# Loads tied to steps of the unit ahead, DMA transposes for units 4 to 10, and new constants in the planner of a fused attention and ReLU-squared kernel

## The chip, the cores and the metric

The kernel runs on one core of one Trainium2 chip. The metric is the device time in microseconds (us) of one execution; lower is better. The inputs and the output lie in HBM as fp32.

## The reference

Two layers follow one another. The first is a gated linear attention over 4 batches, 8 heads, 768 tokens and a head size of 48; the second is a dense block on all 3072 tokens, with 384 inputs, 2048 hidden values and 384 outputs.

```python
for t in range(S):                       # per batch b and head h
    state = alpha[:, :, t, :, None] * state + einsum('bhd,bhe->bhde', k[:, :, t], v[:, :, t])
    y[:, :, t] = einsum('bhd,bhde->bhe', q[:, :, t], state)
x = y.transpose(0, 2, 1, 3).reshape(B * S, H * D)
out = (np.maximum(x @ w_in, 0) ** 2) @ w_out
```

## The kernel before

The work is cut into 12 **units**, numbered g = 0 to 11. A unit is 256 tokens of one batch, all heads; `units = [(b, i) for i in range(NST) for b in range(B)]` takes the first 256 tokens of all four batches, then the second, then the third. For each unit the program adds the following steps, each with a name that the text uses:

- **Loads** `lda`, `ldk`, `ldq`, `ldv`: alpha, k, q and v of the unit, 384 KB each, into one of four `RAW` buffers (L509; unit 0 loads alpha in two halves at L500). Those of unit 1 in part and of unit 2 in whole are issued by POOL, together with the weights `win0`, `win1`, `wout0`, `wout1` (L479); all others are issued by SP. From unit 4 on, the loads of unit g wait until q of unit g-1 has landed (`AFTER`).
- **Front**: the decays. `pr` multiplies pairs of alpha (L618/L620), `ln` and `lm` take logarithms on ACT, `m1i` and `m1s` (L627 to L631) sum them with a triangular matrix on PE, `ei`, `ea`, `ec`, `es` are exponentials on ACT, `bk` and `lb` are small steps on DVE or POOL; `ekm` and `eqm` (DVE, L689) scale k and q; `vc` casts v to bf16.
- **Transposes of scaled k and q**, `tr0` and `tr1`: by PE for units 0 to 2 (L703), by a DMA transpose that SP issues for units 3 to 11 (L716).
- **Scores** `p` (PE, L822) into the PSUM tiles psX and psZ, and the two mask steps `mk0`, `mk1` (DVE, L835).
- **Output** `y` (PE, L759 and L766), which for units 2 to 10 also holds the state products `kv` of the next unit (L739); `sa`, `sb`, `sc`, `sd` update the state. `xe` copies the attention output out of psX (L853/L855).
- **Transpose of the attention output**, `xt`, into one of four `XT` buffers. For units 0 to 7 it is done by PE, in six 128x128 transposes into psX (L868), and `xv` copies the result (DVE, L880). For units 8 to 11 SP issues one DMA transpose (L874) and there is no `xv`.
- **Dense block**: `s1_g_u`, eight groups of six matmuls (L925), reads `XT` and `WIN` and fills one of two PSUM banks; `re` applies the ReLU (ACT L933 or DVE L935), `sq` squares (L943/L947). `s2_g_j_s`, eight groups of four matmuls (L961), multiplies with `WOUT` into the one bank psO; `oe` copies it out (ACT L968 or DVE L970) and `out` stores it (SP, L971). The last 128 rows go through `last_tile` (L895 to L903).

No loop of the kernel sets the order in which these steps stand on an engine. The class `Program` collects them with their reads, writes, estimated durations (`cost`) and priorities (`prio`, built from `FRONT`, `ATTN` and `DENSE`, or 13000 ns times g where a unit has no entry). Its `schedule` plays the steps through with its own constants (`HOP`, the delay of a semaphore; `PE_LATENCY`; `SWITCH`, 95 ns for a change of PE's mode; the DMA constants) and gives every engine a fixed list. A step that has several engines open to it (`alts`) goes to the one that the planner finds free first. `fill` then puts dummy matmuls on PE (L1005, one is 128x256 with zeros) into gaps of over 250 ns that the planner expects before the first `s2`. `place` works out which semaphores each step waits for. On the chip every engine, SP among them, runs its list in that order, and a step that waits holds up all that stands behind it on its engine.

The mode of a PE step, a pair for its beginning and its end, is known to the planner alone: F for steps on the whole array, R for `kv`, T for `p`. Where the mode changes, the planner adds `SWITCH` and may prefer another step of the present mode.

Of the kernel before, what the change touches and what calls it, by code (L numbers as in the profile page):

```python
# [33 lines left out]
class Program:  # L34

    HOP = 70
    PE_LATENCY = 165
    DMA_FIRST = {"sp": 1300, "act": 1300, "pool": 2000}  # L40
    PACKET = (("win", 172), ("wout", 490), ("ld", 22), ("tr", 18), ("xt", 18), ("out", 65))
    SBUF_ONLY = ("pr", "bk", "aq", "ekm", "eqm", "sq", "sb", "sd")
# [58 lines left out]
    def schedule(self):  # L101
# [38 lines left out]
        def land(op, t):  # L140
            op.land = t
            for u in op.users:
# [4 lines left out]
                elif u.deps[op] or e not in u.alts:  # L147
                    ready = t + self.HOP
                else:
# [63 lines left out]
    def fill(self, make, cost, until, gap, after, cold):  # L213


        new = []
        t = after.land + self.HOP
        cold += t
# [115 lines left out]
def bass_gla_recurrent__then__act_relu_squared_kernel(  # L334
# [18 lines left out]
    G = B * NST  # L353
    units = [(b, i) for i in range(NST) for b in range(B)]
    PE_TRANSPOSED = 3
    PE_X = 8
    FRONT = {0: 0, 1: 13000, 2: 26000}
    ATTN = {}
    DENSE = {}
    POOL_LOADS = {1: "v", 2: "akqv"}  # L360
    RATIO = 4
    NRAW, NQKS, NKQT, NPM, NV, NXT, NGT, NRR, NOSB = 4, 3, 3, 2, 4, 4, 2, 4, 4
# [50 lines left out]
    pr = Program(nc)  # L413
    add = pr.add
# [17 lines left out]
    for i in range(2):  # L432
        add("dve", fill(LAF[i][:, :, :, D:64].rearrange("p j h d -> p (j h) d"), 0.0), 250, -1e6 - 10,
            writes=[("laf", i)])
        add("dve", fill(LAB[i][:, :, D:64], 0.0), 150, -1e6 + 20, writes=[("lab", i)])
    for i in range(NQKS):
        add("dve", fill(QKS[i][:, :, :, :, D:64].rearrange("p a j h d -> p (a j h) d"), 0.0), 500, -1e6 + 10,
            writes=[("qks", i, 0), ("qks", i, 1)])
# [8 lines left out]
    for part, key, val in ((HSEL[0:1, 64:128], "hsel", -1000.0), (HSEL[32:33, 0:64], "hsel", -1000.0),  # L447
# [5 lines left out]
        writes=[("ident",)])  # L453

    for c, key in enumerate(("caus", "caus1")):
        add("pool", select(flat[c], ALU.is_ge, 0.0, 128 * c, [[-1, 2], [1, 2], [2, 64]], -2), 400, -1e6 + 7,
            reads=[(key,)], writes=[(key,)])
    add("act", lambda e: e.activation(flat[1][0:64], flat[0][0:64], AF.Copy), 400, -1e6 + 8,
        reads=[("caus",), ("caus1",)], writes=[("caus1",)])
# [23 lines left out]
    load_op = {}  # L483

    def hd(ap):
        return ap.rearrange("p (h d) -> p h d", h=H)

    def load(g):
        b, i = units[g]
        t0 = i * T  # L490
        p0 = g * P
        r, la, qs, kt, pm, vb, x2 = (g % n for n in (NRAW, 2, NQKS, NKQT, NPM, NV, 2))
        first, last = i == 0, i == NST - 1
        sr, sw = 2 * b + i % 2, 2 * b + (i + 1) % 2

        for x in range(2) if g in BY_HEADS else ():
            hs = slice(4 * x, 4 * x + 4)
            src = alpha[b, hs, t0:t0 + T, :].rearrange("h (p j) d -> p h (j d)", j=2)
            dst = RAW[r][:, 0, hs].rearrange("p h j d -> p h (j d)")
            add("sp", lambda e, dst=dst, src=src: e.dma_start(dst, src), 600, L_PRIO[g] + x * 0.5,  # L500
                writes=[("raw", r, 0, x)], name=f"lda{x}_{g}", dma=f"a{r}{x}", lag=615)
        for j, t, nm in ((0, alpha, "a"), (1, k, "k"), (2, q, "q"), (3, v, "v"))[g in BY_HEADS:]:
            src = t[b, :, t0:t0 + T, :].rearrange("h (p j) d -> p h (j d)", j=2)
            dst, key = RAW[r][:, j], ("raw", r, j)
            ring, cost, gate = "sp", 600, AFTER.get((g, nm), AFTER.get(g))
            if nm in POOL_LOADS.get(g, ""):
                ring, cost = "pool", 930
            dst = dst.rearrange("p h j d -> p h (j d)")
            load_op[g, nm] = add(ring, lambda e, dst=dst, src=src: e.dma_start(dst, src), cost, (L_PRIO[g] + j if ring == "sp" else W_PRIO[2] + 10 * g + j),  # L509
                writes=[key], name=f"ld{nm}{g}", dma=f"{nm}{r}{ring}", lag=1230,  # L510
                after=[load_op[gate]] if gate else [])

    def front_by_heads(g, p0):

# [290 lines left out]
    def scores(g):  # L805

        p0 = ATTN.get(g, g * P)
        kt, pm = g % NKQT, g % NPM
# [32 lines left out]
    def output(g, with_state):  # L841
        p0 = ATTN.get(g, g * P)
        x2 = g % 2
        run, cost, reads, writes = output_mm(g)
        if with_state:
            run2, cost2, reads2, writes2 = state_mm(g + 1)
            both = lambda pe, run=run: (run(pe), run2(pe))[1]
            add("pe", both, cost + cost2, p0 + 5600, reads=reads + reads2, writes=writes + writes2, name=f"y{g}",
                mode=("F", "R"))
            state(g + 1, alone=False)  # L850
        else:
            add("pe", run, cost, p0 + 5600, reads=reads, writes=writes, name=f"y{g}", mode=("F", "R"))
        add("act", lambda e: e.activation(XBF[x2][:], psX[:, :, 0:HD], AF.Copy), act_ns(2 * HD), p0 + 6100,  # L853
            reads=[("ps", "X", 0), ("ps", "X", 1)], writes=[("xbf", x2)], name=f"xe{g}",
            alts={"dve": (lambda e: e.tensor_copy(XBF[x2][:], psX[:, :, 0:HD]), dve_ns(2 * HD))})  # L855


        s = g % NXT
        src = XBF[x2][:].rearrange("p c n -> p (c n)")
        dst = XT[s][:].rearrange("p k j t -> p (k j t)")  # L860
        bank = psX[:, 0, :].bitcast(BF16)
        to = bank[:, 0:KT * T].rearrange("p (k j c t) -> p c k j t", k=KT, j=2, c=2)

        def xtr(pe):
            for c in range(2):
                for kk in range(KT):
                    o = c * KT + kk
                    ins = pe.matmul(to[:, c, kk], src[:, o * 128:(o + 1) * 128], IDENT[:], is_transpose=True)  # L868
            return ins

        if g >= PE_X:

            to = XT[s][:].rearrange("p k j t -> p (k j t)").rearrange("p (a t) -> p a t", t=128)
            add("sp", lambda e: e.dma_start_transpose(to, src), 1300, p0 + 6700, reads=[("xbf", x2)],  # L874
                writes=[("xt", s)], name=f"xt{g}", dma=f"x{s}", lag=1400)
            return

        add("pe", xtr, pe_ns(6, 128), p0 + 6700, reads=[("xbf", x2), ("ident",)], writes=[("ps", "X", 0)],
            name=f"xt{g}")
        add("dve", lambda e: e.tensor_copy(dst, bank[:, 0:KT * T]), dve_ns(KT * T, 2),  # L880
            p0 + 7200, reads=[("ps", "X", 0)], writes=[("xt", s)], name=f"xv{g}",
            alts={"act": (lambda e: e.activation(dst, bank[:, 0:KT * T], AF.Copy), act_ns(KT * T))})
# [23 lines left out]
    def moe(g):  # L906
# [3 lines left out]
        p0 = DENSE.get(g, g * P + 20500)  # L910
        nb = FT // per
        for u in range(nb):
            hb, rb, half = h_i[0] % 2, h_i[0] // 2 % NRR, h_i[0] % 2
            h_i[0] += 1
            pu = p0 + u * P * 0.5 / nb

            def s1(pe, u=u, hb=hb):
                for i in range(per):
                    fj = u * per + i
                    for kk in range(KT):  # L920
                        mov = XT[s][:, kk].rearrange("p j t -> p (j t)")
                        if g >= PE_X:
                            mov = XT[s][:].rearrange("p k j t -> p (k j t)").rearrange(
                                "p (c k j t) -> p k j c t", c=2, k=KT, j=2)[:, kk]
                        ins = pe.matmul(psH[hb][:, i * T:(i + 1) * T], WIN[:, kk, hidden(fj)], mov,  # L925
                                        start=(kk == 0), stop=(kk == KT - 1))
                return ins

            fjs = range(u * per, (u + 1) * per)
            add("pe", s1, pe_ns(KT * per, T), pu, reads=[("xt", s)] + sorted({("win", f // FS) for f in fjs}),  # L930
                writes=[("ps", "H", hb)], name=f"s1_{g}_{u}")
            rr = RR[rb][:, half]
            add("act", lambda e, hb=hb, rr=rr: e.activation(rr, psH[hb], AF.Relu), act_ns(512), pu + 600,  # L933
                reads=[("ps", "H", hb)], writes=[("rr", rb, half)], name=f"re{g}_{u}",
                alts={"dve": (lambda e, hb=hb, rr=rr: e.tensor_scalar(rr, psH[hb], 0.0, None, ALU.max),  # L935
                              dve_ns(512))})
            if half == 0 and u < nb - 2:
                continue

            k = 2 if half == 1 and u < nb - 2 else 1  # L940
            dst = GT[gt][:, (u + 1 - k) * per:(u + 1) * per].rearrange("p f j t -> p (f j t)")
            sq = RR[rb][:, half + 1 - k:half + 1].rearrange("p a t -> p (a t)")
            add("dve", lambda e, dst=dst, sq=sq: e.tensor_tensor(dst, sq, sq, ALU.mult), 148 + k * 267, pu + 1200,  # L943
                reads=[("rr", rb, h) for h in range(half + 1 - k, half + 1)],
                writes=[("gt", gt, fj) for fj in range((u + 1 - k) * per, (u + 1) * per)], name=f"sq{g}_{u}",
                alts={"pool": (lambda e, dst=dst, sq=sq: e.tensor_tensor(dst, sq, sq, ALU.mult), 200 + k * 840),
                      "act": (lambda e, dst=dst, sq=sq: e.activation(dst, sq, AF.Square), act_ns(k * 512))})  # L947
        for j in range(2):
# [7 lines left out]
            for sg in range(4):  # L956
                ps_ = p0 + P * 0.5 + 600 + (j * 4 + sg) * P * 0.5 / 8

                def s2(pe, sg=sg, j=j, psS=psS):
# [6 lines left out]
                    reads=[("gt", gt, fj) for fj in range(sg * FT // 4, (sg + 1) * FT // 4)] + [("wout", sg * WS // 4)],  # L966
                    writes=[keyS], name=f"s2_{g}_{j}_{sg}")
            add("act", lambda e, ob=ob, psS=psS: e.activation(OSB[ob][:], psS, AF.Copy), act_ns(DM), ps_ + 700,  # L968
                reads=[keyS], writes=[("osb", ob)], name=f"oe{g}_{j}",
                alts={"dve": (lambda e, ob=ob, psS=psS: e.tensor_copy(OSB[ob][:], psS), dve_ns(DM))})  # L970
            add("sp", lambda e, ob=ob, rows=rows: e.dma_start(out[rows, :], OSB[ob][:]), 600, ps_ + 1300,  # L971
                reads=[("osb", ob)], name=f"out{g}_{j}", dma=f"o{ob}", lag=600)
# [18 lines left out]
    for st in ORDER:  # L991
        kind, g = st[0], int(st[1:])
# [44 lines left out]
```

## Time and profile before

| | before |
|---|---|
| median of 7 runs | 180.3 us (179.91 to 181.14) |
| profiled execution, its own time | 180.38 us |
| its span, first to last instruction | 178.6 us |
| granted TensorE clock | 1.00 |
| busy: PE, PE weight loads, DVE, ACT, POOL | 173.5, 138.3, 121.4, 119.4, 27.9 us |
| SP's DMA queue (q1), share of 16 engines | 63.9% |
| POOL's DMA queue (q0), share of 16 engines | 12.8% |

Busy time is the sum of an engine's instructions in the profile. Matmuls overlap in the record (the next starts before the one ahead has ended), so the work of a PE step is read from the distance between its first start and that of the next step, not from its duration. 1.78 us of the profiled execution lie outside its span.

### The profile page before, as it was taken

The page shows a single profiled execution, that of the slowest core. Times are in us where ns is not written, and L with a number is a line of the kernel's source. Part 1 is how long each engine was busy: PE and PEld are TensorE (multiplying, and loading weights), DVE is VectorE, ACT ScalarE, POOL GpSimd, SP SyncE. Part 2 cuts the span into 40 slices and gives each one's busy share as a digit, 9 for nine tenths or more (in the row PEclk, how much of TensorE's full clock was granted, in tenths as well). Part 3 has the DMA queues.
Part 4 walks back from the last instruction along what each step waited for, and adds up shares of the span by engine and source line. Part 5 has one row for each costly group of instructions (what it writes and reads, how often), then busy time and mean ns, then how long its engine had stood idle before and what let it go on. Part 6 is the DMA issues. An engine that isn't in the chain of part 4 may idle for free.

```text
span 178.6 us, 5262 instructions
## 1 busy us (share of the span) xinstructions
PE 173.5 (97%) x2309; PEld 138.3 (77%) x2309; DVE 121.4 (68%) x197; ACT 119.4 (67%) x214; POOL 27.9 (16%) x35
## 2 busy tenths in 40 slices
PE   7999799999999999999999999999999999999994
PEld 5877698876788788878778878688878787788773
DVE  6579488589867997987889796974738645424130
ACT  5584399598777868949657869566559454656441
POOL 3250751020020301503304331000000000000000
DMA  5999999999999998799999999236132541130112
GB/s 131 305 298 191 215 308 211 238 257 269 248 282 229 299 308 237 180 263 286 258 189 323 223 265 287 74 66 145 48 77 48 132 48 44 48 88 0 46 45 88
DMA packets 72215, 32.59 MB, mean 182 GB/s; under 512 B 67488, under 2 KB 70688, under 8 KB 72192
## 3 DMA queue, kind: packets, MB, share of 16 engines
q1 hardware_dynamic: 70544, 27.14, 63.9%
q0 software_dynamic: 1648, 5.11, 12.8%
q8 instruction: 18, 0.29, 0.7%
q14 instruction: 5, 0.04, 0.1%
HBM read 25.17 MB, written 4.72 MB: 167 GB/s over the span
## 4 chain that ended last, share of the span: by engine, by line
PE 88%; DMA 8%; SPq 2%; issue 0%; ACT 0%
PE psWH L925 37%; PE psO L961 34%; DMA win<-in_moe_w_in_dram 5%; PE psX L766 3%; DMA raw<-in_alpha_dram 3%; PE psX L759 3%; PE psZ L739 2%; PE psX L822 2%; SPq L509 2%; PE psX L895 1%; PE psZ L822 1%; PE psX L868 1%; PE psWH L627 1%; PE psO L1005 1%; SPq L500 1%; PE psZ L703 0%
## 5 line engine op out<-in xcount | busy, mean ns | idle before, releaser
L925 PE MATMUL psWH<-xt,win 128*128 128x256 bf16 x576 | 74.0, 275 | 1.2 <-DMA win<-in_moe_w_in_dram 1.2
L925 PEld LDWEIGHTS psWH<-xt,win 128*128 128x128 bf16 x576 | 65.1, 145 | 6.2 <-issue 1.4
L961 PE MATMUL psO<-wout,gt 128*128 128x384 bf16 x368 | 69.1, 326 | 0.0
L933 ACT ACTIVATE rr<-psWH 128x512 bf16<-128x512 f32 x84 | 49.9, 596 | 25.0 <-PE psWH L925 23.2
L961 PEld LDWEIGHTS psO<-wout,gt 128*128 128x128 bf16 x368 | 34.7, 98 | 18.1 <-DVE gt L943 0.2
L943 DVE TENSOR_TENSOR gt<-rr 128x1024 bf16<-128x1024 bf16 (+1 forms) x42 | 24.6, 589 | 27.1 <-ACT rr L933 26.7
L968 ACT ACTIVATE osb<-psO 128x384 f32<-128x384 f32 x21 | 10.3, 492 | 13.8 <-PE psO L961 13.5
L835 DVE TENSOR_TENSOR pm<-psZ,caus 128x1024 bf16<-128x1024 f32 x12 | 14.6, 1216 | 4.0 <-PE psZ L822 4.0
L835 DVE TENSOR_TENSOR pm<-psX,caus 128x1024 bf16<-128x1024 f32 x12 | 14.6, 1219 | 2.8 <-PE psZ L822 2.8
L947 ACT ACTIVATE gt<-rr 128x1024 bf16<-128x1024 bf16 (+1 forms) x18 | 15.5, 864 | 0.7 <-DVE rr L935 0.4
L1005 PE MATMUL psO<-zero 128*128 128x256 bf16 x76 | 12.3, 310 | 1.2 <-DVE zero L426 1.2
L620 POOL TENSOR_TENSOR prd<-raw 128x384 f32<-128x384 f32 x7 | 7.6, 1088 | 35.2 <-DMA raw<-in_alpha_dram 35.2
L853 ACT ACTIVATE xbf<-psX 128x768 bf16<-128x768 f32 x10 | 8.1, 809 | 6.8 <-PE psZ L739 5.4
L689 DVE TENSOR_TENSOR qks<-raw,ek 128x768 bf16<-128x768 f32 x11 | 10.5, 951 | 0.1
L689 DVE TENSOR_TENSOR qks<-raw,eq 128x768 bf16<-128x768 f32 x11 | 10.5, 950 | 0.0
L935 DVE TENSOR_SCALAR rr<-psWH 128x512 bf16<-128x512 f32 x12 | 8.3, 688 | 2.8 <-PE psWH L925 2.5
L1005 PEld LDWEIGHTS psO<-zero 128*128 128x128 bf16 x76 | 7.9, 110 | 2.9 <-DVE zero L426 1.2
L766 PE MATMUL psX<-vbf,pm 64*128 64x48 bf16 x384 | 6.9, 180 | 0.0
L792 DVE TENSOR_TENSOR tmp<-psZ,sbd 128x384 f32<-128x384 f32 x8 | 4.4, 552 | 3.4 <-PE psZ L739 3.4
L685 POOL CAST vbf<-raw 128x768 bf16<-128x768 f32 x4 | 4.6, 1153 | 13.3 <-DMA raw<-in_v_dram 10.3
L639 ACT ACTIVATE ek<-psWH 128x384 f32<-128x384 f32 x10 | 4.9, 489 | 2.1 <-PE psWH L627 1.1
L766 PEld LDWEIGHTS psX<-vbf,pm 64*128 64x128 bf16 x384 | 5.6, 93 | 0.8
(119 smaller groups left out, 170.7 us busy)
## 6 DMA issues: line engine op xcount, KB each, us to landing
out_dram<-osb SPq DMA_DIRECT2D x23, 192.0 KB, 3.4
raw<-in_k_dram SPq DMA_DIRECT2D x11, 384.0 KB, 4.5
raw<-in_q_dram SPq DMA_DIRECT2D x11, 384.0 KB, 5.0
raw<-in_v_dram SPq DMA_DIRECT2D x10, 384.0 KB, 5.1
raw<-in_alpha_dram SPq DMA_DIRECT2D x10, 384.0 KB, 4.4
win<-in_moe_w_in_dram POOLq DMA_DIRECT2D x2, 768.0 KB, 10.1
wout<-in_moe_w_out_dram POOLq DMA_DIRECT2D x2, 768.0 KB, 9.1
raw<-in_v_dram POOLq DMA_DIRECT2D x2, 384.0 KB, 5.7
```

Of the source, the lines that this page charges most:

```text
L689: add("dve", lambda e, a=a, E=E: e.tensor_tensor(QKS[qs][:, a, :, :, 0:D], RAW[r][:, 1 + a].rearrange("p h j d -> p j h d"), E[la][:].rear ...
L766: ins = pe.matmul(psX[:, c, h * D:(h + 1) * D], PM[pm][64 * c:64 * c + 64, n // 2, rr_, n % 2, jk, :], VBF[vb][64 * c:64 * c + 64, h, jk, ...
L835: add("dve", lambda e, hf=hf, psT=psT: e.tensor_tensor(PM[pm][:, hf].rearrange("p r n j t -> p (r n) (j t)"), psT[:, :, :].rearrange("p r ...
L853: add("act", lambda e: e.activation(XBF[x2][:], psX[:, :, 0:HD], AF.Copy), act_ns(2 * HD), p0 + 6100, reads=[("ps", "X", 0), ("ps", "X", 1 ...
L925: ins = pe.matmul(psH[hb][:, i * T:(i + 1) * T], WIN[:, kk, hidden(fj)], mov, start=(kk == 0), stop=(kk == KT - 1))
L933: add("act", lambda e, hb=hb, rr=rr: e.activation(rr, psH[hb], AF.Relu), act_ns(512), pu + 600, reads=[("ps", "H", hb)], writes=[("rr", rb ...
L935: alts={"dve": (lambda e, hb=hb, rr=rr: e.tensor_scalar(rr, psH[hb], 0.0, None, ALU.max), dve_ns(512))})
L943: add("dve", lambda e, dst=dst, sq=sq: e.tensor_tensor(dst, sq, sq, ALU.mult), 148 + k * 267, pu + 1200, reads=[("rr", rb, h) for h in ran ...
L947: "act": (lambda e, dst=dst, sq=sq: e.activation(dst, sq, AF.Square), act_ns(k * 512))})
L961: ins = pe.matmul(psS, GT[gt][:, fj, j, :], WOUT[:, fj, :], start=(fj == 0), stop=(fj == FT - 1))
L968: add("act", lambda e, ob=ob, psS=psS: e.activation(OSB[ob][:], psS, AF.Copy), act_ns(DM), ps_ + 700, reads=[keyS], writes=[("osb", ob)], ...
L1005: pr.fill(lambda pe: pe.matmul(psO[:, 0:256], ZERO[:, 0:128], ZERO[:, 0:256], skip_group_check=True), 109, min(o.start for o in pr.order[" ...
```

## The change

Four things change in the program's text.

1. Every load of a unit g of 5 or more waits, besides what it waited for before, for a step of unit g-1: alpha for `ln`, k for the landing of `tr0`, q and v for the landing of `tr1`. SP itself does the waiting.
2. The attention output is transposed by DMA for units 4 to 10. Units 4 to 7 go from PE to DMA, unit 11 from DMA to PE.
3. The planner's constants are others: `HOP` 35 for 70, `PE_LATENCY` 170 for 165, the beginning of `y` gets a mode of its own (C), and `FRONT`, `ATTN` and `DENSE` have entries for the first units and for the dense block of unit 11.
4. Since the planner makes the lists, all engines' lists are new from the middle of unit 0 on.

```diff
-    HOP = 70
-    PE_LATENCY = 165
+    HOP = 35
+    PE_LATENCY = 170
...
-    PE_X = 8
-    FRONT = {0: 0, 1: 13000, 2: 26000}
-    ATTN = {}
-    DENSE = {}
+    DMA_X = (4, 5, 6, 7, 8, 9, 10)
+    FRONT = {0: 0, 1: 15124, 2: 28243, 3: 27962, 4: 36918, 5: 52460}
+    ATTN = {1: 12619, 2: 26150, 3: 37152, 4: 50460}
+    DENSE = {0: 20223, 1: 32105, 2: 46275, 3: 57124, 11: 158500}
...
+    def named(x):
+        return next(o for o in pr.ops if o.name == x)
+
+    BEHIND = {"a": "ln", "k": "tr0_", "q": "tr1_", "v": "tr1_"}
+
...
-                after=[load_op[gate]] if gate else [])
+                after=([load_op[gate]] if gate else []) + ([named(f"{BEHIND[nm]}{g - 1}")] if g >= 5 else []))
...
-                mode=("F", "R"))
+                mode=("C", "R"))
...
-            add("pe", run, cost, p0 + 5600, reads=reads, writes=writes, name=f"y{g}", mode=("F", "R"))
+            add("pe", run, cost, p0 + 5600, reads=reads, writes=writes, name=f"y{g}", mode=("C", "R"))
...
-        if g >= PE_X:
+        if g in DMA_X:
...
-                        if g >= PE_X:
+                        if g in DMA_X:
```

What the diff alone does not show is the order. In the changed program a late unit has this list on SP (unit 8 to 9; out5 is a store of unit 5):

```
tr0_8, lda9, out5_0, tr1_8, ldk9 (waits for tr0_8's landing), out5_1,
xt7 (waits for xe7), ldq9 (waits for tr1_8's landing), ldv9, tr0_9, ...
```

and this on PE, from one output to the next:

```
y7 with kv8, s1_6_3, s1_6_4, s2_6_0_0, s1_6_5, s1_6_6, m1i9, s2_6_0_1, s1_6_7, s2_6_0_2,
p8, s1_7_0 (waits for xt7), s2_6_0_3, s1_7_1, s1_7_2, s2_6_1_0 to s2_6_1_3, y8 with kv9
```

DVE has `ekm9`, `mk0_8`, `eqm9` (waits for ldq9), `mk1_8` in that order, and y8 waits for `mk1_8` and for `vc9`. Before, the front of unit 9 stood on PE at 101 us and `p` of unit 9 at 125 us; now a unit's front lies about one unit ahead of its scores. Of the dummy matmuls behind the first `s1`, 12 become 7.

## The prediction

> **What bounds the kernel now.** I read the page's busy shares first, then the list of waits for PE alone, the chain that ended last, PE's timeline, and the costliest groups.
>
> ```profile
> PE 173.5 (97%) x2309; PEld 138.3 (77%) x2309; DVE 121.4 (68%) x197; ACT 119.4 (67%) x214; POOL 27.9 (16%) x35
> ...
> PE 88%; DMA 8%; SPq 2%; issue 0%; ACT 0%
> ...
> L868 PE MATMUL psX<-ident,xbf 128*128 128x128 bf16 x48 | 4.0, 219 | 0.1
> ```
>
> ```profile
> PE psO L1005 <- DVE zero L426: 1.2, 1, 1.2
> PE psWH L925 <- DMA win<-in_moe_w_in_dram: 1.2, 1, 1.2
> ```
>
> The second fence is all that PE waited for in 178.6 us: the zero tile at the start, and the first half of w_in, which lands at 18.8 us and lets `s1_0_0` begin at 18.94. From there on PE is a full queue: the chain is 88% PE, and in PE's timeline the steps follow at distances that repeat to a few ns. **No load, no transpose and no copy holds PE back after 19 us.** So waiting that is saved in SP's queue or on DVE saves nothing by itself; the time falls only by work that leaves PE's list, and rises by new work or new waits there.
>
> The distances, from PE's timeline: an `s1` group 0.655 us, an `s2` group 0.650, `p` 0.573, `y` with `kv` 1.311 from unit 4 on, and a transpose of the attention output 0.335, here:
>
> ```profile
> 70.95 0.50 PE L868 MATMUL psX<-ident,xbf 128*128 128x128 bf16 x6
> 71.29 1.46 PE L961 MATMUL psO<-wout,gt 128*128 128x384 bf16 x8
> ```
>
> A full-array step ahead of `p`, `kv` or `y` takes 0.093 more; one behind them takes 0.058 more if it is `s1` and 0.010 if it is `s2`. Added up in the order of before, from 18.94 on, these give 175.17 us for the end of the last matmul group; it ended at 176.02. **0.85 us of small waits** are in it, none over 0.15: 0.43 beside the dummy matmuls and `s1_1_1` and `s1_1_2`, the rest mostly at `s2_2_0_3` and its neighbours.
>
> **What the Trainium skill says.** *Perfetto Trace Analysis*, section "Identifying the Most-Contended Engine", warns that PE's busy share is no measure of its limit, since pipelined matmuls overlap in the record; so I use distances. *TensorE: Matmul & The Clock Gate*, "Back-to-back issue gap", gives 262 cycles for 256 columns, 109 ns at its 2.4 GHz; the trace agrees (six in 0.655 us). *DMA: Bandwidth & Descriptors*, "Anatomy of one DMA", says that DMA engines never wait on a semaphore, that the issuing sequencer does. The trace has such waits on SP (22.8 us for wout before `lda3`), so each added wait holds all that SP has behind it.
>
> **Part by part.**
>
> *PE's own work.* (a) `xt` leaves PE for units 4 to 7 and comes back for unit 11: 3 x 0.335 = -1.01 us. (b) Dummy matmuls behind `s1_0_0`: 12 to 7, -0.45 (five at 0.109, less 0.093, as one now stands ahead of `y1`). (c) Neighbours: eight more `p` and `y` are followed by `s1` instead of `s2`, and some groups change sides: `s1` +0.16, `s2` +0.12, short `m1` -0.09. The same sum in the new order ends at 173.91: **-1.26 us**. The matmuls read a DMA-made XT with another stride; for units 8 to 11 of before their distance is the same 0.655, so that costs nothing.
>
> *Other engines.* `xv` (DVE, 0.556 each) goes for a net three units, -1.67 us on DVE, which is 68% busy and has no part in the chain: nothing. SP issues three more DMA transposes of about 1.25 us; SP's own cost is hidden while the transfers behind them land in time.
>
> *The load gates.* They delay loads; PE waits for no load before, so they gain nothing in themselves and can only cost. What they change is the traffic: before, loads ran far ahead and kept the DMA engines at 101 to 116% of their time from 19 to 100 us, and DMA transposes landed like this, first all of `tr0` and `tr1` (L716), then those issued from 110 us on, with the loads over, then `xt` (L874), which before runs only in that quiet stretch:
>
> ```profile
> DMA to landing us min/median/max: 3.0/4.0/6.2
> ...
> DMA to landing us min/median/max: 3.0/3.1/4.6
> ...
> DMA to landing us min/median/max: 2.8/2.9/3.3
> ```
>
> Loads (L509) landed 3.6 to 6.4 us after issue, median 5.0. The trace of before shows no `xt` among loads: between 2.9 (quiet) and 6.2 (the worst `tr`). I take 2.9 to 4, since the same loads are now spread over about 12.8 us for a unit instead of about 9 (from `lda5` at 48.0 us to `lda11` at 101.9, six units).
>
> *Does each added wait end in time?* Late units, with t = 0 at the start of `y7` and a period of 12.79 us (8 x 0.655 + 8 x 0.650 + 1.311 + 0.573 + 0.162 + edges):
> - `y7` ends at 1.31. In unit 9 of before `xe` began 1.41 us after `y` did and SP issued `xt` 2.25 us after, so `xt7` goes out at 2.3 and lands at 5.2 (8.5 at worst). `s1_7_0` is due at 7.42: **2.2 us of slack**, and a landing over 5.1 us after issue stops PE.
> - `ldq9` stands behind `xt7`: issued at 3.6, landed at 8.6. DVE runs `mk0_8` from 7.5 to 8.7 (the mask began 0.69 us behind `p`'s start before), `eqm9` to 9.6, `mk1_8` to 10.8; `y8` is due at 12.79. Slack 2.0 us; `ldq9` may take 7.0 us. `ldv9`, issued about 0.7 later, lands at 9.3; `vc9` on POOL (up to 1.5) ends by 10.8: the same slack.
> - `ldk9` waits for `tr0_8` and holds up out5_1 and `xt7`. `tr0_8` was issued some 7 us before; even 6.2 is in time. The stores need not be prompt: `oe` waits for the store two units back.
>
> The first gated units are tighter. `tr0_4` and `tr1_4` need no longer stand behind three loads of unit 5 and go out at about 49.3 and 50.6 instead of 53.3 and 54.7. `ldq5` follows `tr1_4`'s landing at 54.5 to 55.5 and lands by 60.5; `eqm5`, `mk0_4`, `mk1_4` (0.87 + 1.14 + 1.21) end by 63.8, `y4` is due at about 65. `ldq6` goes out behind `xt4` at 68.3 and lands at 73.3; `es6` ends at about 74.0 on ACT, `eqm6` and `mk1_5` at 76.1, `y5` is due at 76.9: **0.7 us, the smallest slack of the attention steps**.
>
> *New small waits.* `m1s2` and `s1_1_2`: ACT now has `re0_7` ahead of `ei2` to `ec2`, +0.35. `s2_0_1_0`: only `kv2` (0.446) lies between it and `s2_0_0_3`, while `oe0_0` needs 0.2 + 0.49 to free psO's one bank: +0.25. With 0.35 for small ones elsewhere (before had 0.42 outside its early gaps) that is 0.95, against 0.85 before: +0.10, from -0.5 (hardly any wait left) to +2.
>
> *Sum.* Against the profiled execution: span 178.6 - 1.26 + 0.10 = 177.4, with 1.78 outside it 179.2. That execution (180.38) lies 0.08 above the median of 180.3, so I forecast **179.2 us**, 0.6% faster. About 0.3%, 0.54 us, is what a measurement of this kernel can tell from no change.
>
> **Rivals.**
> - *The gain is eaten by small waits* (18%). The place is DVE: `mk1` stands behind `eqm` of the next unit, which waits for a load that starts late. For it: 0.7 us of slack at `y5`, and one ACT or DVE step placed otherwise uses it up. Against: 2 us in the later units. If seven outputs wait 0.15 each, 1.05 of 1.26 is gone: 180.2.
> - *DMA transposes of the output land late* (12%): slower. `s1_g_0` of units 4 to 10 now waits for SP's list and for a landing. From 5.1 us after issue on, every 0.1 us costs 0.7 us over seven units. For it: the eight `tr` transposes issued from 42 to 80 us had a median of 4.9. Against: that was behind queued loads, and `xt` is issued ahead of `ldq` and `ldv`, with `ldk` mostly landed. At 5.5 us: +2.8 - 1.2, about 181.9.
> - *All waits go* (8%): the work of PE alone, 180.3 - 1.26 - 0.6 = 178.4.
> - *The change does not do what it says*: that the gates speed the transposes up is likely, but PE waits for none, so the forecast stands on (a) to (c) even then.
>
> **How the numbers follow.** The forecast has 62%: 178.7 to 179.7. The range 178.5 to 180.7 adds most of the first rival and half of the third, and leaves out the slow one. Faster by over 0.3%: 62 + 8 = 70%; within 0.3%: 17%; slower: 13% (the late transposes and the far end of the eaten gain).
>
> **What would show it.** Right: 30 instead of 48 matmuls at L868, seven at L874 landing in about 3 to 4 us, still no DMA in PE's list of waits but w_in, PE's last group ending near 174.9, DMA share below 100% from 60 us on. Wrong: PE waits for `xt` ahead of L925, or for DVE `pm` ahead of L759; a longer distance of `s1`; or an end of PE no earlier than 176.0.

## The result, and the profile after

The changed kernel takes **178.99 us** (median of 13 runs, 178.29 to 180.1) against 180.5 for the kernel before (34 runs beside it): a ratio of **0.9914**, 95% interval 0.9895 to 0.9932. Measured again, among other runs, it took 179.33 against 180.43: 0.9944 (0.9919 to 0.9968). So the two measurements put the gain at 0.9% and at 0.6%, and their intervals overlap between 0.9919 and 0.9932; the forecast was 0.6%. The profiled execution has a span of 177.4 us and 179.19 us in all.

The changed file is five lines longer, so that L868 of before is L873, L874 is L879, L716 is L721, L925 is L930 and L961 is L966.

The page of the changed kernel, with the busy shares and the chain that ended last by engine, and then, from the list of groups, the transposes that stay on PE (x30 is their number; 2.5 us busy, 219 ns each).

```profile
span 177.4 us, 5228 instructions
PE 171.6 (97%) x2287; PEld 136.6 (77%) x2287; DVE 121.2 (68%) x197; ACT 120.0 (68%) x211; POOL 26.6 (15%) x35
...
PE 88%; DMA 7%; SPq 2%; issue 1%; ACT 0%
```

```profile
L873 PE MATMUL psX<-ident,xbf 128*128 128x128 bf16 x30 | 2.5, 219 | 0.2 <-ACT xbf L858 0.2
```

PE is still the bound at 97%, and its matmuls fell from 2309 to 2287: 18 fewer transposes (48 to 30) and four fewer dummies (five go behind `s1_0_0`, one more stands ahead of it). The answer on PE's waits shows whom PE waited for, with the total, the number and the longest, in us:

```profile
PE psO L1010 <- DVE zero L426: 1.3, 1, 1.3
PE psWH L930 <- DMA win<-in_moe_w_in_dram: 0.9, 1, 0.9
PE psZ L579 <- DVE qks L567: 0.6, 1, 0.6
PE psX L873 <- ACT xbf L858: 0.2, 1, 0.2
```

All four lie ahead of or at `s1_0_0`; behind it the list names nothing, and the waits of 0.1 to 0.2 that follow show only in the distances. Seven transposes by DMA are there, and PE waits for none of them. The next answers give, for `tr0` and `tr1` (L721) and for `xt` (L879), the time from issue to landing; in the line of L879, 1211/1229/2090 is how long one transpose held SP, in ns (least, median, most):

```profile
DMA to landing us min/median/max: 3.1/4.1/6.3
...
L879 SPq DMA_TRANSPOSE xt<-xbf x7: 1211/1229/2090, 67.7 to 144.0; - x7
DMA to landing us min/median/max: 2.7/3.6/4.5
```

So the loads did not keep `xt` from landing within 4.5 us, against the 5.1 at which PE would have stopped. `tr` is no faster than before (median 4.1 for 4.0): the gates do not speed it up.

The view by stretches has the length, the busy us of PE, PEld, DVE, ACT and POOL with instruction counts, the granted clock, the DMA engines' share and the GB/s. First the kernel before, then after:

```profile
60.00:100.00 40.00, 40.00 (x564) 32.16 (x565) 35.18 (x52) 29.87 (x57) 9.75 (x8) 1.00 1.08 262
100.00:140.00 40.00, 40.00 (x553) 31.87 (x551) 29.10 (x43) 27.29 (x48) 4.20 (x4) 1.00 0.61 127
```

```profile
60.00:100.00 40.00, 40.00 (x569) 32.14 (x558) 33.08 (x49) 29.94 (x55) 5.03 (x5) 1.00 0.98 207
100.00:140.00 40.00, 40.00 (x522) 31.68 (x520) 28.47 (x41) 30.04 (x53) 4.96 (x5) 1.00 0.96 209
```

The same loads are now spread evenly: 207 and 209 GB/s instead of 262 and 127. The DMA engines are busier from 100 us on, and PE is at 40.00 of 40 us in all four rows: traffic is what the gates change (with the gates alone it is 199 and 196 GB/s), and PE does not see it.

**Where the time came from.** The first `s1` group began at 18.61 us instead of 18.94, since w_in landed sooner (-0.33). From there, the sum of PE's distances in the new list is 1.26 shorter, as forecast; the small waits in it are 1.17 us instead of 0.84 (+0.33). The last half group therefore starts at 173.40 instead of 174.68. The landing of w_in varied by itself: over the 14 profiled executions of this study `s1_0_0` began between 17.83 and 20.18 us, and everything behind it moves with it. To compare profiles I use the **PE stretch**, from the start of `s1_0_0` to the start of the last half group, which leaves that out: 155.73 before, 154.80 after, 154.57 in the second profile of after.

### The profile page after: what moved, and what is told of

It is laid out like the page before. It is cut to its first block, busy times and chain, and to the rows that moved or that the text cites. A ratio compares the mean times of both kernels' runs of the same rounds, so it can differ in the third digit from the quotient of the medians.

```text
span 177.4 us, 5228 instructions
## 1 busy us (share of the span) xinstructions
PE 171.6 (97%) x2287; PEld 136.6 (77%) x2287; DVE 121.2 (68%) x197; ACT 120.0 (68%) x211; POOL 26.6 (15%) x35
## 4 chain that ended last, share of the span: by engine, by line
PE 88%; DMA 7%; SPq 2%; issue 1%; ACT 0%
PE psWH L930 38%; PE psO L966 34%; DMA win<-in_moe_w_in_dram 5%; PE psX L771 3%; DMA raw<-in_alpha_dram 3%; PE psX L764 3%; PE psX L827 2%; PE psZ L744 2%; SPq L514 2%; PE psX L900 1%; PE psZ L827 1%; PE psWH L632 1%; PE psX L873 1%; PE psZ L708 1%; SPq L505 1%
## 5 line engine op out<-in xcount | busy, mean ns | idle before, releaser
L930 PE MATMUL psWH<-xt,win 128*128 128x256 bf16 x576 | 74.4, 275 | 0.9 <-DMA win<-in_moe_w_in_dram 0.9
L930 PEld LDWEIGHTS psWH<-xt,win 128*128 128x128 bf16 x576 | 65.0, 145 | 5.9 <-DVE kqt L715 0.9
L966 PE MATMUL psO<-wout,gt 128*128 128x384 bf16 x368 | 69.0, 326 | 0.1
L966 PEld LDWEIGHTS psO<-wout,gt 128*128 128x128 bf16 x368 | 35.3, 98 | 17.8 <-ACT osb L973 0.3
L973 ACT ACTIVATE osb<-psO 128x384 f32<-128x384 f32 x20 | 9.8, 492 | 11.6 <-PE psO L966 11.1
L858 ACT ACTIVATE xbf<-psX 128x768 bf16<-128x768 f32 x11 | 8.9, 812 | 6.1 <-PE psZ L744 4.7
L1010 PE MATMUL psO<-zero 128*128 128x256 bf16 x72 | 11.1, 303 | 1.3 <-DVE zero L426 1.3
L690 POOL CAST vbf<-raw 128x768 bf16<-128x768 f32 x6 | 5.8, 964 | 41.2 <-DMA raw<-in_v_dram 41.2
L1010 PEld LDWEIGHTS psO<-zero 128*128 128x128 bf16 x72 | 7.4, 108 | 2.7 <-DVE zero L426 1.3
L940 DVE TENSOR_SCALAR rr<-psWH 128x512 bf16<-128x512 f32 x11 | 7.5, 686 | 1.7 <-PE psWH L930 1.6
L806 POOL TENSOR_TENSOR sbd<-tmp,acm 128x384 bf16<-128x384 f32 x4 | 4.2, 1050 | 18.4 <-DVE tmp L804 18.4
```

Source lines behind the costliest of these rows:

```text
L966: ins = pe.matmul(psS, GT[gt][:, fj, j, :], WOUT[:, fj, :], start=(fj == 0), stop=(fj == FT - 1))
L1010: pr.fill(lambda pe: pe.matmul(psO[:, 0:256], ZERO[:, 0:128], ZERO[:, 0:256], skip_group_check=True), 109, min(o.start for o in pr.order[" ...
```

## The experiments

Three parts can be put in separately: **D**, the DMA transposes for units 4 to 10; **G**, the gates on the loads; **P**, the planner's constants, FRONT, ATTN, DENSE and the mode of `y`. The planner makes new lists each time, so the six kernels with some of the parts are also six orders. In the tables "sum" is the end of the last matmul group by PE's distances alone, in the way of the prediction, and "waits" is what PE lost beside it, both in us; before has 175.17 and 0.84. (The sum is counted as if `s1_0_0` began at 18.94 in each.)

### D, G and P alone

```diff
# D alone (b_dmax), against before
-    PE_X = 8
+    DMA_X = (4, 5, 6, 7, 8, 9, 10)
...
-        if g >= PE_X:
+        if g in DMA_X:
...                                    # and the same in s1
```
```diff
# G alone (b_gates), against before: named(), BEHIND and
-                after=[load_op[gate]] if gate else [])
+                after=([load_op[gate]] if gate else []) + ([named(f"{BEHIND[nm]}{g - 1}")] if g >= 5 else []))
```
```diff
# P alone (b_plan), against before: FRONT, ATTN, DENSE and
-    HOP = 70
-    PE_LATENCY = 165
+    HOP = 35
+    PE_LATENCY = 170
...
-                mode=("F", "R"))
+                mode=("C", "R"))
```

> Kernel before with one edit: units 4 to 10 transposed by DMA, the planner making a new order with its old constants. My theory (PE's list is the bound, so only work that leaves it counts): the sum of PE's distances from 18.94 us ends at 174.11 instead of 175.17, so -1.06 us, 179.4 us, ratio 0.994. Rival (the gates are needed, because loads that run ahead make the transposes land late): PE waits for xt or for tr, and the gain is smaller than 0.5 us or a loss.

> Kernel before with the load gates alone. My theory: PE waits for no load and no transpose before, so nothing is gained; PE's sum ends at 175.26, +0.09; 180.5 us, the same. Rival (thinner traffic is worth something in itself): -0.5 us or more.

> Kernel before with the planner's new constants alone (HOP, PE_LATENCY, the mode of y, FRONT, ATTN, DENSE). My theory: PE's sum ends at 174.77, -0.40 (five dummy matmuls fewer, short m1 and neighbours about even), and the early waits cost up to 0.3 more: -0.1 to -0.4 us, about 180.2, hardly to be told from before. Rival (the order made with measured latencies is the main thing): -1 us or more.

| | us | before beside it | ratio (95%) | sum | waits |
|---|---|---|---|---|---|
| D | 185.01 | 180.12 | 1.0267 (1.0229 to 1.0304) | 174.11 | 5.81 |
| G | 180.37 | 180.12 | 1.0016 (0.9995 to 1.0038) | 175.26 | 1.10 |
| P | 180.69 | 180.12 | 1.0028 (1.0007 to 1.0049) | 174.77 | 1.82 |

G does what the prediction said of the gates: nothing that can be measured. P takes 0.40 from the sum, nearly all of it the five dummies, and pays 0.98 in waits. Some 0.7 of that lies before 42 us, beside the dummies that are left and at `s2_0_1_0` and `y2` (0.20 each); there P's PE list is that of the changed kernel, which has these waits too. The rest lies mostly at `s1_3_0` and `s1_3_2` (0.17 and 0.20). D was a clear miss of mine. Its sum fell by 1.06, and it is 2.7% slower. PE's waits in D:

```profile
PE psO L961 <- ACT osb L968: 1.6, 3, 0.6
PE psO L1005 <- DVE zero L426: 1.3, 1, 1.3
PE psWH L925 <- DMA win<-in_moe_w_in_dram: 1.0, 1, 1.0
PE psWH L627 <- ACT lab L621: 0.7, 1, 0.7
PE psX L759 <- DVE pm L835: 0.4, 1, 0.4
PE psO L961 <- DVE gt L943: 0.4, 1, 0.4
```

No DMA but w_in is among them: `xt` went out up to 10.6 us behind `y` and landed in 2.8 to 5.5, and still no `s1` waited for it, since the planner had put `s1` later. The largest line is of a kind that before hardly had: PE for `osb`, the copy that empties psO. In D's PE list `s2_g_0_3`, the last group of the first half of a unit, and `s2_g_1_0`, the first of the second half, stand side by side in units 3 and 4; both need psO's one bank. Each pair lost 0.74 to 0.75 us. The third wait for `osb` is of the same kind: in unit 6 only a short `m1i11` lies between the halves, and 0.58 is lost. In after's list 1.3 us of other matmuls lie between them in every unit but the first. The two pairs and unit 6 make 2.1 of the 5.0 us of waits that D adds. The largest single wait is another, 0.80 at `m1i10`, and it leads back to a load: `lda10` went out at 96.8 and landed at 100.5, POOL's `pr10` stood idle for it, and `ln10` and `m1i10` come behind `pr10`. So PE's list of waits does not name the load, but a load was late here at second hand.

```profile
100.56 1.33 POOL L620 TENSOR_TENSOR prd<-raw 128x384 f32<-128x384 f32 x1 [2.74 <-DMA raw<-in_alpha_dram]
```

### D with P, G with P, D with G

```diff
# D with P (a_nogate), against after
-... if g >= 5 else []))
+... if g >= 50 else []))
```
```diff
# G with P (a_pex), against after
-    DMA_X = (4, 5, 6, 7, 8, 9, 10)
+    DMA_X = (8, 9, 10, 11)
```
```diff
# D with G (b_gates_dmax), against after: FRONT, ATTN, DENSE as before and
-    HOP = 35
-    PE_LATENCY = 170
+    HOP = 70
+    PE_LATENCY = 165
...
-                mode=("C", "R"))
+                mode=("F", "R"))
```

> Changed kernel without the gates; the planner makes another order in which loads run ahead again. My theory: PE's sum ends at 173.70, 0.21 less than with gates, and nothing waits on PE: within 0.3 us of the changed kernel, about 178.8. Rival (gates needed): xt and tr land late behind loads, PE waits for DMA, 0.5 us or more slower than the changed kernel.

> Changed kernel with the transposes of the output as before (PE for units 0 to 7, DMA for 8 to 11). My theory: PE's sum ends at 174.77 instead of 173.91, so +0.86 us against the changed kernel: 179.9 us. Rival (order and gates make the gain): within 0.3 us of the changed kernel.

> Kernel before with gates and DMA transposes, and the old planner constants. New theory (the loss of DMA transposes without gates comes from the list: the planner expects xt late behind queued loads, puts s1_g_0 late, and leaves the two halves of s2 side by side on the one bank psO): with gates the list has 1.3 us between the halves in all units, PE's sum ends at 174.31, so -0.86 us and few waits: 179.3 us, ratio 0.994 to 0.996. Rival (the new constants are needed too): no faster than before.

| | us | before beside it | ratio (95%) | sum | waits |
|---|---|---|---|---|---|
| D, P | 183.65 | 180.12 | 1.0194 (1.0153 to 1.0234) | 173.70 | 5.42 |
| G, P | 182.49 | 180.06 | 1.0134 (1.0096 to 1.0172) | 174.77 | 3.22 |
| D, G | 180.06 | 180.43 | 0.9978 (0.9954 to 1.0001) | 174.31 | 1.98 |
| D, G, P (after, second time) | 179.33 | 180.43 | 0.9944 (0.9919 to 0.9968) | 173.91 | 0.96 |

Taking the gates out of the changed kernel costs 2.8 points (1.0194 against 0.9914), where I had expected nothing. PE's waits without them:

```profile
PE psO L966 <- ACT osb L973: 1.2, 2, 0.6
PE psWH L930 <- DMA xt<-xbf: 0.7, 2, 0.4
PE psO L966 <- ACT gt L952: 0.4, 2, 0.2
```

Two pairs on psO stand side by side (units 4 and 5, 0.75 and 0.76 in PE's distances), and there are two waits for `xt`, 0.57 and 0.48 in the distances. Without gates SP's list puts `xt` behind up to four loads of later units: in units 4 to 7 it goes out 5.8 to 9.3 us behind `y` instead of 2.3. Pairs and `xt` make 2.6 of the 4.5 us of waits that come on top of after's.

G with P is slower by more than the 0.86 of PE work that comes back. Its largest waits are 0.74 at `s2_8_0_3`, for a square that the planner gave to POOL in this list, and 0.61 at `s1_9_0`, for `xt9`. That one is the slow rival of the prediction at a single place: `xt9` took 6.3 us from issue to landing, over the 5.1 at which PE stops, though the gates are there. SP had issued two loads just ahead of it:

```profile
134.08 0.42 SPq L514 DMA_DIRECT2D raw<-in_q_dram  x1
134.56 0.69 SPq L514 DMA_DIRECT2D raw<-in_v_dram  x1
135.29 2.44 SPq L879 DMA_TRANSPOSE xt<-xbf  x1
```

```profile
DMA to landing us min/median/max: 2.8/3.5/6.3
```

Over all 14 profiles, the 24 transposes of the output that SP issued right behind `ldk` landed in 2.8 to 4.7 us; the six right behind `ldv`, the last load of a unit, took 4.5 to 6.3. (Those right behind a store or another transpose took 2.7 to 4.5, and one 5.3.) This points to the place on SP's list, ahead of `q` and `v`, as what keeps `xt` quick in the changed kernel; no run moves an `xt` behind `ldv` and nothing else, so it is not shown apart.

D with G has no wait for `xt` and no pair side by side, and ends at 0.9978: the gates take the whole loss of D away. The gain that I had expected of it, 0.994 to 0.996, did not come in full: its interval reaches 1.0001, so it is not shown to be faster than before. With the constants as well it is 179.33 instead of 180.06 in the same set of runs, 0.40 of it by the sum; the two intervals just overlap.

### The order without the waits

Do the gates help as waits, or only through the list that the planner makes with them? Here all engines' lists are those of after, and the gates' waits are left out after planning:

```diff
# a_order_nowait, against after
+    gates = []
...
+            if g >= 5:
+                gates.append((load_op[g, nm], named(f"{BEHIND[nm]}{g - 1}")))
...
+    for o, d in gates:
+        o.deps.pop(d)
```

> Changed kernel with every engine's order kept, and only the semaphore waits of the gates left out (their loads still stand behind the same steps in SP's list). My theory: within 0.2 us of the changed kernel, since loads go out only 0.5 to 2 us earlier and PE waits for none of it. Rival (the waiting itself protects the transposes from queued loads): xt lands 1 us or more later, PE waits for it at units 5, 6 and 9, where the changed kernel has 0.8 to 1.0 us of slack, and the time rises by 0.5 us or more.

179.26 us against 180.06, **0.9953** (0.9933 to 0.9974), and a PE stretch of 154.79 for 154.80. PE's waits and the landing of `xt`:

```profile
PE psO L1013 <- DVE zero L426: 1.2, 1, 1.2
PE psWH L933 <- DMA win<-in_moe_w_in_dram: 0.4, 1, 0.4
PE psX L876 <- ACT xbf L861: 0.2, 1, 0.2
```

```profile
DMA to landing us min/median/max: 2.7/3.6/4.5
```

So the waits are worth nothing that can be measured, in either direction: after itself had 0.9914 and 0.9944. The traces show why. In after SP hardly waits at the gates; of its waits, this one line is theirs for certain, 1.8 us in all:

```profile
SPq L514 <- DMA kqt<-qks: 1.8, 3, 0.7
```

I had expected that without the waits the loads would go out 0.5 to 2 us earlier. Measured from the `y` two units ahead, only `ldk6` did (0.72); no other load of units 5 to 11 went out more than 0.22 earlier. What holds `ldq` and `ldv` back is SP's list itself: they stand behind `xt`, and `xt` waits for `xe`. So this run shows that in this list the waits do no work; it does not show what loads that run ahead would do to `xt`. What D without G lacks is a good list: planned with the gates, `q` and `v` of a later unit stand behind `xt`, and without them all four loads can stand ahead of it.

### Two s2 halves side by side

One suspected cost of D by itself: in after's PE list, for units 4 to 9, the two `s1` groups between the halves are moved behind the second half. The same matmuls run, and the lists of all other engines stay.

```diff
# a_adj, against after
+    for g in range(4, 10):
+        at = pe.index(named(f"s2_{g}_0_3"))
+        group = pe[at + 1:at + 7]
+        assert [o.name for o in group] == [f"s1_{g + 1}_1", f"s1_{g + 1}_2"] + [f"s2_{g}_1_{s}" for s in range(4)]
...
+        for k, (o, t) in enumerate(zip(group[2:] + group[:2], starts)):
+            pe[at + 1 + k], o.start, o.pos = o, t, at + 1 + k
...
```

> Changed kernel with one move on PE for g = 4 to 9: s1_(g+1)_1 and s1_(g+1)_2 go behind the second half of s2 of unit g, so that s2_g_0_3 and s2_g_1_0, which share psO, stand side by side. All other lists and PE's work stay the same. New theory: each of the six pairs waits about 0.75 us for oe, as in the kernels without gates: +4.5 us, about 183.4. Rival (such pairs are a sign of a list that is late for other reasons, not a cause): under 1 us.

184.7 us against 180.43: **1.0218** (1.0177 to 1.026). The waits of PE have grown to 6.86 us: six of 0.75, which is the 4.5 that I had expected, and four of 0.20 to 0.37 behind them, which I had not.

```profile
PE psO L966 <- ACT osb L973: 3.5, 6, 0.6
...
PE psWH L930 <- ACT rr L938: 0.4, 2, 0.2
```

The list of waits gives 0.58 for one, the idle time at the matmul; the distances give 0.75, since a matmul's modelled end covers the rest. The timelines of a_adj show one handover, first PE, then ACT (start, duration, engine and line, idle time ahead):

```profile
99.91 0.81 PE L966 MATMUL psO<-wout,gt 128*128 128x384 bf16 x4
101.30 0.99 PE L966 MATMUL psO<-wout,gt 128*128 128x384 bf16 x5 [0.58 <-ACT osb L973]
```

```profile
100.75 0.49 ACT L973 ACTIVATE osb<-psO 128x384 f32<-128x384 f32 x1
```

`s2_5_0_3` ends at 100.72, the copy runs from 100.75 to 101.24, and `s2_5_1_0` starts at 101.30: 1.39 us from group to group instead of 0.65. The same place in after's PE timeline:

```profile
98.75 0.81 PE L966 MATMUL psO<-wout,gt 128*128 128x384 bf16 x4
99.40 1.47 PE L930 MATMUL psWH<-xt,win 128*128 128x256 bf16 x12
100.71 2.76 PE L966 MATMUL psO<-wout,gt 128*128 128x384 bf16 x16
```

Two `s1` groups, 1.31 us, cover the copy, and nothing waits. The Trainium skill, *PSUM — Partial Sum Buffer*, "Terms", says that TensorE writing a bank while another engine reads it is an error, so a kernel with one bank must wait for its copy; the run agrees with the order (the next matmul starts 0.06 us behind the copy), and none here shows what would happen otherwise. This makes the pairs of D (two, 1.49 us) and of D with P (two, 1.51) a shown cost of those lists, about a third of what they add in waits; their other waits, most of them 0.2 to 0.8 each, I read from the traces and did not isolate.

### A late xt

Two spare DMA transposes of the same data into unused buffers, ahead of each of the seven `xt` on SP; the lists are otherwise those of after.

```diff
# a_xd2, against after
+            for n in range(2):
+                xd = XD[2 * (g % 3) + n][:].rearrange("p k j t -> p (k j t)").rearrange("p (a t) -> p a t", t=128)
+                add("sp", lambda e, xd=xd: e.dma_start_transpose(xd, src), 0, p0 + 6700 - 2 + n, ...)
```

> Changed kernel with two spare DMA transposes of the same size (into buffers that nobody reads) issued by SP directly ahead of each of the seven xt; all other orders are the same. In the changed kernel xt landed 0.80 to 2.45 us before s1_g_0 needed it. My theory (late xt stops PE one for one): each xt lands about 2.5 us later, waits of 0.7, 1.7, 1.5, 0.1, 0.9, 1.7 and 0.3 us in units 4 to 10, together 6.9: about 185.9 us. Rival (PE has other work to overlap, or xt was never close): under 1 us.

189.7 us against 180.06: **1.0532** (1.0484 to 1.058), 3.8 us more than I had expected.

```profile
PE psWH L935 <- DMA xt<-xbf: 5.8, 6, 1.2
PE psWH L935 <- DMA win<-in_moe_w_in_dram: 2.0, 1, 2.0
PE psX L765 <- DVE pm L841: 1.4, 2, 1.1
PE psX L765 <- POOL vbf L691: 0.5, 1, 0.5
```

`xt` went out 4.84 to 5.59 us behind `y` instead of 2.25, and landed 7.7 to 8.55 us behind it. The prediction had `s1_g_0` due at 7.42. So PE stopped in all seven units, for 0.20 to 1.26 us, 6.54 in all, close to the 6.9 that I had expected. That the due time of the walk is the real edge is what this run shows; the slow rival was a real mechanism, and it did not happen because `xt` is issued and lands in time. What my expectation left out is the queue: `ldq` stands behind `xt` on SP, and `y` of four units waited for its mask or `vc`, 2.30 us together. Some 1.5 us of the distances lie at 21 to 25 us, where this execution was granted a TensorE clock of 0.59, and are no part of the mechanism.

The Trainium skill, *DMA: Bandwidth & Descriptors*, "Issuing engines are not separate DMA queues", says that the time to start a DMA is usually small beside the DMA. Here the measurement decides otherwise: one transpose holds SP for 1.2 us (the 1229 ns above) and lands in 2.7 to 4.5. Two spare ones made `xt` go out 2.6 to 3.3 us later, while `xt` itself still landed 2.8 us (median) after its issue.

### More units by DMA

```diff
# a_x3_11, against after
+    DMA_X = (3, 4, 5, 6, 7, 8, 9, 10, 11)
# a_x11, against after
+    DMA_X = (4, 5, 6, 7, 8, 9, 10, 11)
```

> Changed kernel with units 3 and 11 transposed by DMA as well. My theory: two more PE transposes go, PE's sum ends at 173.09, -0.82 us against the changed kernel: 178.2 us. In unit 11 the first s1 stands 6.3 us behind y11 and needs xt at about 5.2, close; if it lands over 4 us after issue PE waits. Rival: a wait for xt at unit 3 or 11 eats it, 179.0 or more.

> Changed kernel with unit 11 transposed by DMA too. The list keeps 1.3 us between the halves of s2 in every unit from 1 on. PE's sum ends at 173.57, -0.34 us against the changed kernel; xt11 is needed 6.3 us behind y11 and would land at about 5.1: 178.6 us, if xt11 is in time. Rival: PE waits for xt11 and the time is the same or worse.

Units 3 and 11 as well: 179.2 against 180.06, 0.9957 (0.9934 to 0.998). The sum fell by 0.82 to 173.09, but in this list `s2_2_0_3` and `s2_2_1_0` stand side by side, and one wait of 0.75 takes it back; I had expected 178.2.

Unit 11 as well, without unit 3: **178.8** against 180.43, 0.9891 (0.9847 to 0.9935), the lowest median of the study. The sum is 173.57 (-0.34, one transpose), the waits 1.06, the PE stretch 154.35, 0.22 below the second profile of after; `xt11` landed 0.95 us before it was needed. Its interval and that of after (0.9919 to 0.9968) overlap, so by time alone it is not shown to be faster than after; against before it is.

The changed kernel once more, with nothing edited (after2):

> The changed kernel once more, unaltered, beside the other kernels of this set: about 0.99 of before, and the same as with the gates' waits left out.

179.33 us, waits 0.96, stretch 154.57, as in the tables.

## Why the prediction was right

- **PE sets the time, and only its list and its waits count.** Right: DVE makes five copies of the transposed output instead of eight, at 0.55 us each, and POOL is busy 1.3 us less; neither shows in the end.
- **The PE sum, -1.26.** Right: with it and the 0.33 more of waits the profiled stretch is 0.93 shorter by the sum, 0.94 by the trace.
- **The new small waits.** At `s2_0_1_0` 0.25 was forecast and 0.20 measured. At `m1s2` and `s1_1_2` 0.35 was forecast; 0.16 and 0.10 came beside the dummies, with 0.16 at `s1_1_4` and 0.20 at `y2`, which were not on the list. In all they are 1.17 and 0.96 in the two profiles, for 0.95. Not one is later than 42 us, so the first rival, 0.15 at each of seven outputs, did not come up.
- **`xt` in time.** It was issued 2.25 to 2.33 us behind `y`, for 2.3; it landed 4.97 to 6.75 behind it, for 5.2 and 8.5 at worst; the slack was 0.80 to 2.45, for 2.2. The transposes landed in 2.7 to 4.5, for the 2.9 to 4 taken. That this is what held the slow rival off is shown by the run with the late `xt`. The reason given for it, that `xt` is issued ahead of `ldq` and `ldv`, fits with `xt9` of G with P, which stood behind them and took 6.3.
- **`y5` as the tightest step.** Its mask ended at 77.08 and it started at 77.75: 0.67 for 0.7, though both came almost 1 us later than the walk had them.
- **The gates and the transposes.** One side remark was wrong: the prediction called it likely that the gates speed the transposes up, and `tr` took as long as before. As it said, nothing hung on that.
- **The span.** It is 177.4 us, as forecast. This is partly luck: the first `s1` group began 0.33 sooner, which no term had, and that stands against +0.33 of waits where +0.10 was forecast; the stretch behind the start of the last half group is 3.96 us before and 3.97 after.

Where the reasoning was too simple: it priced the parts as if each were worth its own term. "They gain nothing in themselves" holds for G alone (1.0016) and for the waits as such (no measurable difference without them). It does not follow that the change could do without them. No part gains alone, and D loses 2.7% without G: the gates work through the planner, which without them queues `xt` behind loads and moves groups, so that psO halves meet (about a third of the loss, shown) and PE waits elsewhere (read from the traces). Likewise term (b), -0.45 for the dummies, is real in the sum, but the list that comes with it costs more: P alone has 0.98 us more of waits. The prediction got the total right because it was worked out from the order of the changed kernel, in which all of this had been settled.

Still open: which of the constants in P brings the last 0.3%; which of the three is behind each of the smaller waits in G with P; and whether the 0.3% between the two measurements of after is more than noise, since their intervals overlap; a scatter in w_in's landing is one possible cause, not shown to be the one.

## What to carry to other kernels

When a planner makes the lists, price a change from the lists it yields, not from the edit: sum the bound engine's distances in the new order, then walk each due time. Look for two users of a single PSUM bank that have come to stand side by side; here each such pair costs 0.75 us, more than two transposes on PE. Moving a small transpose to DMA pays as long as its consumer is due later than the issue delay plus the slowest landing in that place of the queue (here 2.3 + 4.5 of 7.4 us; right behind a unit's last load it was up to 6.3), and on the issuing queue it also delays all that stands behind it.

## What was not expected of the hardware

- The time at which the half of w_in lands that starts PE scatters widely: the first `s1` group began between 17.83 and 20.18 us over the 14 profiled executions, though SP's and POOL's lists begin with the same loads in the same order; in 13 of them PE's waits name w_in as the last to come, for 0.4 to 2.0 us. That is more than the whole gain of the change, and a reason to compare PE stretches rather than spans.
- In the changed kernel DMA transposes of the output took 2.7 to 4.5 us amid loads at a DMA share of 0.96 to 0.98, against 2.8 to 3.3 with hardly any loads in the kernel before. The load on the DMA engines alone does not set it: in D with G, at shares of 0.88 and 0.94, all seven took 2.7 to 2.8. In other lists the same transpose took up to 6.3, as much as the slowest `tr`, and the slow ones are mostly those issued right behind a unit's last load.
